# Sliding-window attention and a dropless mixture of experts: rows of a slot turned by VectorE in 32x32 blocks, over buckets with another order of columns

## The chip, the cores and the metric

The kernel runs on one core of a Trainium2 chip. A time is the device time of one execution in microseconds (us). Below, PE is TensorE (its weight loads are listed apart as PEld), DVE is VectorE, ACT is ScalarE, POOL is GpSimd and SP is SyncE, which here only issues DMAs.

## The reference

Everything is in fp32. There are 8 batches of 8 heads with 576 positions of 64 values. Attention is causal and sparse: in heads 0 to 3 a query sees the last 32 keys, in heads 4 to 7 every fourth one of the last 128.

```python
scores = scale * np.matmul(q, k.transpose(0, 1, 3, 2))
mask_plain = (rel >= 0) & (rel < 32)
mask_dil = (rel >= 0) & (rel < 128) & (rel % 4 == 0)
attn = softmax(where(mask, scores, -1e9));  out = attn @ v
```

The heads of one token are put side by side, which makes 4608 rows of 512 values (512 = 8 heads x 64). Each row goes to one of 8 experts, the one with the largest logit, and is weighted with its softmax probability:

```python
logits = x @ w_gate;  expert_idx = np.argmax(logits, axis=1)
gate_w = probs[np.arange(N), expert_idx]
y[rows of e] = np.maximum(x[rows of e] @ w1[e], 0.0) @ w2[e]      # 512 -> 1024 -> 512
return gate_w[:, None] * y
```

## The kernel before

**Attention.** The work is cut into 32 units: for each batch two types of head, and for each type two pairs of heads. A unit turns q and k (`turn`), makes scores in bands of 96 keys (`front`), exponentials on ACT, the division on POOL (`norm`), turns the weights (`weights`, whose tile `eT` DVE copies from PSUM) and sums the values (`summed`). The result `xT` of a unit holds 128 of a token's 512 values, on partitions, by 576 tokens. `row_part` turns it back on PE into rows (`xrow`), and ACT (L574) and DVE (L577) copy these into the tile `rows`, 514 values per token: the 512 values, the weight of the gate and the token's number.

**Routing.** When a batch has ended, `route` finds each token's expert and its rank in it, and POOL scatters the rows with indirect DMAs into `bucket`, a DRAM tensor with a region for each expert. `tables` then computes, for the slots of that stage, which expert a slot has, where its 128 rows begin (`base`) and whether it needs new weights (`new`).

**Slots.** The expert layers run in slots of 128 rows of one expert, up to 41 of them. Two slots, called mixed, hold rows of two experts, in four groups of G = 32. For each slot:

- `fetch_x` reads 128 rows of 514 values from the bucket into the tile `x` (four buffers), with one DMA (four in a mixed slot). SP issues it for the first 26 slots, ACT for later ones; there it is ordered after the last ReLU of ACT (`evicted`).
- `fetch_w` reads the expert's w1 and w2 in four DMAs of 1 MB, on SP's queue, if the expert is new. There are two buffers, and a half is asked for when the slot that used it last has passed the place where it reads it. The list `wanted` fixes the order of the fetches, and `done` counts how far the slots have come.
- `across` turns the slot's rows: four transposes on PE into one PSUM bank, and one copy by DVE to the tile `xt` (two buffers), with the 512 values on partitions in four chunks of 128. It is called for the next slot between the two halves of `ph` (in a mixed slot, in the middle of `py`).
- `ph` is x @ w1 for 8 chunks of 128 hidden values, in two halves; ACT applies the first ReLU and DVE the second. Each half is 16 matmuls of 128x128 by 128 columns, which the trace lists as 32 (L1239).
- `py` is h @ w2, 8 matmuls into 512 columns (16 in the trace, L1271). ACT scales the result with the row's gate (L1282), DVE turns the token number into an integer (L1285) and POOL scatters the rows to the output (L1288).

In a mixed slot the operands change places: `xt` is the stationary one, by groups of 32 columns (`grouped`, L1201), and the hidden rows are turned on PE (`turned_h`).

**Order.** Slots are interleaved with attention by hand. `moe` is a generator that yields the estimated cost of what it has issued (0.93 for the four matmuls of a chunk of ph, 0.88 for a chunk of py, 0.5 for `across`), and `run_slots` at the end of the program lets it run at a rate that makes a stage's slots, `SLOT` each, end with the attention that runs beside them. Within an engine, `tc.issue_after` adds an order where it is wanted: the first DVE instruction of `norm` comes after the last turned tile (`crossed`). Slots from number 36 on are in branches that are only taken if the slot has rows.

Of the kernel before, what the change touches and what calls it, by code (L numbers as in the profile page):

```python
# [12 lines left out]
F32 = mybir.dt.float32  # L13
I32 = mybir.dt.int32
BF16 = mybir.dt.bfloat16
AF = mybir.ActivationFunctionType
# [20 lines left out]
ROW = DM + 2  # L37
# [126 lines left out]
def kernel(  # L164
# [398 lines left out]
    def row_part(b, c, xT):  # L563

        if c == 2:
            rows[b] = pool.tile([TT, NT, ROW], F32, tag="rows", name=f"rows_{b}")
            logits[b] = lpsum.tile([128, TT + REST], F32, tag="logits", name=f"logits_{b}")
            nc.gpsimd.tensor_scalar(
                rows[b][:, :, DM + 1], const("tok", TT), float(b * S), None, op0=OP.add
            )  # L570
        ps, row = bank("xrow", 4, 128), rows[b][:, :, 128 * c : 128 * c + 128]
        for i in range(NT - 1):
            nc.tensor.transpose(ps[:, i], xT[:, TT * i : TT * i + TT], ident)  # L573
        nc.scalar.copy(row[:, 0 : NT - 1], ps)  # L574
        ps = bank("xrow")[0:REST, 0:128]
        nc.tensor.transpose(ps, xT[:, S - REST : S], ident)
        nc.vector.tensor_copy(row[0:REST, NT - 1], ps)  # L577

    def logit_part(b, c, xT):

# [490 lines left out]
    w1s = cpool.tile([128, 2, 4, F], F32, name="w1")  # L1071
    w2s = cpool.tile([128, 2, 8, DM], F32, name="w2")
    mixed = {J0 + at0: i for i, at0 in enumerate(MIX)}
    xs, guards, evicted = {}, ExitStack(), []

    def fetch_x(j):
        b, n, _, basei, _ = where[j]
        x = xs[j] = mpool.tile([128, ROW], F32, tag="x", name=f"x_{j}", bufs=4)
        with ExitStack() as order:


            queue = nc.sync
            if j >= J0 + 2:
                queue = nc.scalar
                if j < SURE:
                    order.enter_context(tc.issue_after(evicted[-1].ins))
            if j in mixed:
                for g in range(4):
                    a = 2 * NMIX + 4 * mixed[j] + g
                    at0 = queue.value_load(  # L1090
                        mix["ints"][:, a : a + 1], min_val=0, max_val=NROWS - G
                    )
                    read_bucket(queue.dma_start(x[G * g : G * g + G], bucket[ds(at0, G), :]), b)
            else:
                at0 = queue.value_load(basei[:, n : n + 1], min_val=0, max_val=E * CAP)
                read_bucket(queue.dma_start(x, bucket[ds(at0, 128), :]), b)

    regs = {}

# [65 lines left out]
    def moe():  # L1165


        def across(j):
            ps = bank("xt", 4, 128)
            for c in range(4):  # L1170
                nc.tensor.transpose(ps[:, c], xs[j][:, 128 * c : 128 * c + 128], ident)  # L1171
            xt = mpool.tile([128, 4, 128], F32, tag="xt", name="xt")
            crossed.append(nc.vector.tensor_copy(xt, ps))  # L1173
            return xt

        late, xt = [], None
        for j in range(NSLOT):
# [5 lines left out]
            if j >= SURE:  # L1183
# [2 lines left out]
                guards.enter_context(tc.If(live[0] > j))  # L1186
                while late:
                    late.pop(0)()
            x = xs[j]
            if xt is None:  # L1190
                xt = across(j)
                yield 0.5
            h = mpool.tile([128, 8, 128], F32, tag="h", name="h")
            w1, w2 = w1s[:, j % 2], w2s[:, j % 2]
            nxt = None
# [1 line left out]
            def grouped(out, lhsT, ws, cols, c, n, j=j):  # L1197

                for g in range(4):
                    mine = slice(G * g, G * g + G)  # L1200
                    nc.tensor.matmul(  # L1201
                        out[mine],
                        lhsT=lhsT[:, mine],
                        rhs=ws[:, (j + (g >= KIND[mixed[j]])) % 2, c, cols],
                        start=c == 0,
                        stop=c == n - 1,
                    )

            def turned_h(hrow, fg):
                ps = bank("ht", 4, 128)  # L1210
                for fi in range(4):
                    nc.tensor.transpose(ps[:, fi], hrow[:, fi], ident)
                (nc.scalar.copy, nc.vector.tensor_copy)[fg](h[:, 4 * fg : 4 * fg + 4], ps)

            hrows = []
            for fg in range(2) if j in mixed else ():
                ph = bank("ph")
                for c in range(4):
                    grouped(ph, xt[:, c], w1s, slice(512 * fg, 512 * fg + 512), c, 4)
                    if (fg, c) == (1, 1):  # L1220
                        turned_h(hrows[0], 0)
                    yield 0.93
                hrow = mpool.tile([128, 4, 128], F32, tag="xt", name="hrow")
                flat = hrow.rearrange("p i f -> p (i f)")
                done[0] = 2 * j + fg + 1
                if fg == 0:
                    evicted.append(nc.scalar.activation(flat, ph, AF.Relu))
                    while late:
                        late.pop(0)()
                else:  # L1230
                    relu = nc.vector.tensor_scalar(flat, ph, 0.0, None, op0=OP.max)
                fetch()
                hrows.append(hrow)
            for fg in range(2) if j not in mixed else ():
                ph = bank("ph", 4, 128)
                for fi in range(4):
                    f = 4 * fg + fi
                    for c in range(4):
                        nc.tensor.matmul(  # L1239
                            ph[:, fi],  # L1240
                            lhsT=w1[:, c, 128 * f : 128 * f + 128],
                            rhs=xt[:, c],
                            start=c == 0,
                            stop=c == 3,
                        )
                    if fi < 3:
                        yield 0.93
                done[0] = 2 * j + fg + 1
                if fg == 0:
                    evicted.append(nc.scalar.activation(h[:, 0:4], ph, AF.Relu))  # L1250
                    while late:
                        late.pop(0)()
                    fetch()
                    yield 0.93
                    if j + 1 in xs:
                        nxt = across(j + 1)
                        yield 0.5
                else:
                    relu = nc.vector.tensor_scalar(h[:, 4:8], ph, 0.0, None, op0=OP.max)  # L1259
                    fetch()  # L1260
                    yield 0.93
            py = bank("py")
            for f in range(8):
                if j in mixed:
                    if f == 2:
                        turned_h(hrows[1], 1)
                    if f == 4 and j + 1 in xs:
                        nxt = across(j + 1)
                    grouped(py, h[:, f], w2s, slice(0, DM), f, 8)
                else:  # L1270
                    nc.tensor.matmul(py, lhsT=h[:, f], rhs=w2[:, f], start=f == 0, stop=f == 7)  # L1271
                if f == 3:
# [6 lines left out]
            else:  # L1279
                y = mpool.tile([128, DM], F32, tag="yo", name="y")  # L1280
                to = mpool.tile([128, 1], I32, tag="to", name="to", bufs=6)
            nc.scalar.activation(y, py, AF.Copy, scale=x[:, DM : DM + 1])  # L1282

            with tc.issue_after(relu.ins):
                nc.vector.tensor_copy(to, x[:, DM + 1 : ROW])  # L1285

            def scatter(y=y, to=to):
                i = nc.gpsimd.indirect_dma_start(  # L1288
# [21 lines left out]
    slots, routing = moe(), []  # L1310
    clock = {"moe": 0.0, "all": 0.0, "owed": 0.0, "rate": 0.0}
    ready = []
    SLOT = 0.5 + 8 * 0.93 + 8 * 0.88


    ATT, BEHIND = 32.0, 12.0
# [77 lines left out]
```

## Time and profile before

| what | value |
|---|---|
| median of 3 runs | 776.44 us (770.65 to 779.24) |
| profiled execution | 830.33 us |
| its span | 828.5 us |
| PE busy | 773.6 us, 93% |
| DVE / ACT / POOL busy | 274.4 / 229.1 / 146.3 us |
| mean granted PE clock | 0.956 |
| moved by DMA | 195.42 MB, mean 236 GB/s |
| slots that ran | 35 ordinary, 2 mixed |

The page gives the busy time of each engine, the chain of work that ended last (followed back from the last instruction to what released it each time), and groups of instructions by line with busy time, mean duration and the idle time ahead of them. Matmuls are pipelined: the duration in a record is longer than the time by which the next one starts, so the time that PE needs for a piece is read from start to start. A tile's own view gives its instructions, what its engine waited for and who waited for the tile.

### The profile page before, as it was taken

The page shows a single profiled execution, that of the slowest core. Times are in us where ns is not written, and L with a number is a line of the kernel's source. Part 1 is how long each engine was busy: PE and PEld are TensorE (multiplying, and loading weights), DVE is VectorE, ACT ScalarE, POOL GpSimd, SP SyncE. Part 2 cuts the span into 40 slices and gives each one's busy share as a digit, 9 for nine tenths or more (in the row PEclk, how much of TensorE's full clock was granted, in tenths as well). Part 3 has the DMA queues.
Part 4 walks back from the last instruction along what each step waited for, and adds up shares of the span by engine and source line. Part 5 has one row for each costly group of instructions (what it writes and reads, how often), then busy time and mean ns, then how long its engine had stood idle before and what let it go on. Part 6 is the DMA issues. An engine that isn't in the chain of part 4 may idle for free.

```text
span 828.5 us, 18147 instructions
## 1 busy us (share of the span) xinstructions
PE 773.6 (93%) x6870; PEld 574.1 (69%) x6870; DVE 274.4 (33%) x963; ACT 229.1 (28%) x853; POOL 146.3 (18%) x142
## 2 busy tenths in 40 slices
PE   6997997998999899989999899969999999999993
PEld 4776775886777677767777677646777466577681
DVE  3674765664343433443341311135110110101010
ACT  4985663552333233222331010000100101000010
POOL 4424333113111311130110200060000000000000
PEclk9998979898999899998999989978999999999997
DMA  7985679998998968796406818978994292883996
GB/s 184 208 194 162 139 187 323 294 264 265 358 269 294 305 189 243 245 303 232 132 26 223 261 59 289 327 241 295 313 335 149 93 317 99 318 313 138 324 312 213
DMA packets 177053, 195.42 MB, mean 236 GB/s; under 512 B 71249, under 2 KB 103137, under 8 KB 176963
## 3 DMA queue, kind: packets, MB, share of 16 engines
q1 hardware_dynamic: 166960, 169.01, 65.8%
q0 software_dynamic: 7248, 21.43, 7.2%
q10 hardware_dynamic: 2754, 3.78, 1.4%
q8 instruction: 57, 0.93, 0.5%
q14 instruction: 34, 0.27, 0.1%
HBM read 216.16 MB, written 21.54 MB: 287 GB/s over the span
## 4 chain that ended last, share of the span: by engine, by line
PE 85%; issue 5%; ACT 5%; DVE 1%; another core or an unknown queue 1%; DMA 1%; POOLq 0%; ACTq 0%; POOL 0%; DVEq 0%
PE ph L1239 31%; PE py L1271 29%; PE xo L469 5%; PE weights L454 3%; PE scores L388 3%; ACT e L425 3%; PE turned L342 2%; PE xt L1171 2%; PE ph L1201 2%; PE py L1201 2%; PE logits L583 2%; PE xrow L573 2%; PE turned L351 2%; DMA k<-in_k_dram 1%
## 5 line engine op out<-in xcount | busy, mean ns | idle before, releaser
L1239 PE MATMUL ph<-xt,w 128*128 128x128 f32 x2240 | 276.4, 280 | 4.1 <-issue 3.1
L1239 PEld LDWEIGHTS ph<-xt,w 128*128 128x128 f32 x2240 | 267.3, 196 | 18.0 <-issue 15.7
L1271 PE MATMUL py<-w,h 128*128 128x512 f32 x560 | 262.5, 609 | 3.9 <-issue 3.9
L1271 PEld LDWEIGHTS py<-w,h 128*128 128x128 f32 x560 | 102.8, 194 | 107.9 <-issue 105.9
L1288 POOL DMA_INDIRECT out_dram<-y,to x35 | 34.8, 993 | 412.0 <-ACT y L1282 326.6
L1173 DVE COPY xt<-xt 128x512 f32<-128x512 f32 x38 | 26.3, 691 | 211.1 <-PE xt L1171 205.8
L1282 ACT ACTIVATE y<-py,x 128x512 f32<-128x512 f32 x35 | 24.0, 687 | 223.0 <-PE py L1271 181.4
L444 POOL TENSOR_TENSOR e<-e,rec 128x864 f32<-128x864 f32 x32 | 52.2, 1631 | 142.2 <-DVE rec L443 121.7
L456 DVE COPY eT<-weights 96x384 f32<-96x384 f32 x96 | 47.3, 545 | 58.6 <-PE weights L454 44.9
L469 PE MATMUL xo<-eT,v 96*64 96x64 f32 (+1 forms) x1216 | 51.6, 233 | 13.7 <-issue 13.6
L469 PEld LDWEIGHTS xo<-eT,v 96*64 96x64 f32 x1216 | 44.1, 144 | 21.0 <-issue 16.6
L425 ACT ACTIVATE e<-e,lo 128x96 f32<-128x96 f32 x144 | 51.8, 362 | 12.0 <-DVE lo L417 10.9
L425 ACT ACTIVATE e<-scores,lo 128x96 f32<-128x96 f32 (+1 forms) x160 | 52.4, 345 | 2.3 <-DVE lo L404 1.9
L239 POOL DMA_INDIRECT bucket<-rows,idx x40 | 39.0, 975 | 56.0 <-DVE idx L671 37.3
L1259 DVE TENSOR_SCALAR h<-ph 128x512 f32<-128x512 f32 x35 | 24.1, 688 | 73.5 <-PE ph L1239 73.5
L334 ACT COPY kT<-turned 128x288 f32<-128x288 f32 x64 | 22.5, 403 | 86.0 <-PE turned L342 44.0
L1250 ACT ACTIVATE h<-ph 128x512 f32<-128x512 f32 x35 | 20.9, 596 | 89.9 <-PE ph L1239 73.7
L454 PE MATMUL weights<-ident,e 128*96 128x128 f32 x288 | 39.3, 281 | 3.0 <-issue 2.0
L454 PEld LDWEIGHTS weights<-ident,e 128*96 128x96 f32 x288 | 32.2, 129 | 10.4 <-issue 8.1
L388 PEld LDWEIGHTS scores<-kT,qT 64*64 64x64 f32 x1152 | 31.8, 143 | 9.7 <-issue 4.0
L388 PE MATMUL scores<-kT,qT 64*64 64x96 f32 x1152 | 36.8, 260 | 1.2 <-ACT kT L334 1.0
L410 DVE TENSOR_TENSOR e<-scores,masks 128x384 f32<-128x384 f32 x64 | 23.0, 399 | 33.7 <-PE scores L388 18.1
(220 smaller groups left out, 612.5 us busy)
## 6 DMA issues: line engine op xcount, KB each, us to landing
w<-in_moe_w_dram SPq DMA_DIRECT2D x164, 1024.0 KB
x<-bucket SPq DMA_DIRECT2D x26, 257.0 KB
v<-in_v_dram SPq DMA_DIRECT2D x32, 192.0 KB
q<-in_q_dram SPq DMA_DIRECT2D x32, 144.0 KB
v<-in_v_dram SPq DMA_DIRECT2D x48, 96.0 KB
k<-in_k_dram SPq DMA_DIRECT2D x28, 144.0 KB
x<-bucket ACTq DMA_DIRECT2D x11, 257.0 KB
q<-in_q_dram SPq DMA_DIRECT2D x14, 192.0 KB
```

What stands on the lines that cost most here:

```text
L239: nc.gpsimd.indirect_dma_start(out=bucket, out_offset=bass.IndirectOffsetOnAxis(ap=idx, axis=0), in_=rows, in_offset=None, bounds_check=NR ...
L388: nc.tensor.matmul(sc[r][64 * c : 64 * c + 64, 96 * (i % 5) : 96 * (i % 5) + 96], lhsT=qT[rows, 64 * j : 64 * j + 64], rhs=kT[rows, first_ ...
L425: nc.scalar.activation(out=e[p0:p1, i], in_=s[:, 96 * (i - i0) : 96 * (i - i0) + 96], func=AF.Exp, bias=lo[p0:p1, i : i + 1], scale=-1.0, ...
L444: return nc.gpsimd.tensor_tensor(out=e, in0=e, in1=rec.unsqueeze(2).broadcast_to([128, 9, 96]), op=OP.mult)
L454: nc.tensor.transpose(tp[0:96, 128 * i : 128 * i + 128], e[:, a + i], ident)
L456: nc.vector.tensor_copy(eT, tp[0:96, 0:384])
L469: nc.tensor.matmul(xo[DH * h : DH * h + DH, at0 : at0 + nq], lhsT=vt[:, 2 * hl + r, j, :] if ty == 0 else vt[:, hl, j, DH * r : DH * r + D ...
L1173: crossed.append(nc.vector.tensor_copy(xt, ps))
L1201: nc.tensor.matmul(out[mine], lhsT=lhsT[:, mine], rhs=ws[:, (j + (g >= KIND[mixed[j]])) % 2, c, cols], start=c == 0, stop=c == n - 1,)
L1239: nc.tensor.matmul(ph[:, fi], lhsT=w1[:, c, 128 * f : 128 * f + 128], rhs=xt[:, c], start=c == 0, stop=c == 3,)
L1271: nc.tensor.matmul(py, lhsT=h[:, f], rhs=w2[:, f], start=f == 0, stop=f == 7)
L1288: i = nc.gpsimd.indirect_dma_start(out=out, out_offset=bass.IndirectOffsetOnAxis(ap=to, axis=0), in_=y, in_offset=None, bounds_check=N - 1 ...
```

## The change

An ordinary slot's rows are turned by DVE, with `nc.vector.transpose`, in place of four transposes on PE and a copy. DVE's transpose turns each block of 32x32 by itself, so the rest of the turning is put into the layout:

- `row_part` writes the columns of a row in another order. Value 128 c + 32 i + d (chunk c, quarter i of the chunk) goes to column 128 i + 32 c + d. A quarter i of all four chunks then lies side by side, 128 values.
- `fetch_x` reads an ordinary slot's rows in four pieces, one for each i: partitions 32 i to 32 i + 31 get the piece i of all 128 rows, as four groups g of 32 rows (partition t of the 32 holds the rows 32 g + t). These are descriptors of 512 bytes. Gate and token number come with a fifth DMA into a tile of their own, `tail`.
- `across` is then one DVE instruction over 128 partitions and 512 columns, SBUF to SBUF. Its result is ordered by group, chunk and row in the group, so `ph` reads its moving operand as four runs of 32 columns with a stride of 128 columns.
- A mixed slot keeps PE's transposes. ACT first puts its columns back into the old order (tile `order`), and its DMAs are eight in place of four.
- The yields of 0.5 for `across` are gone, and so is their share of `SLOT`.

```diff
-        ps, row = bank("xrow", 4, 128), rows[b][:, :, 128 * c : 128 * c + 128]
+        ps = bank("xrow", 4, 128)
+        row = rows[b][:, :, 0:DM].rearrange("p n (i q d) -> p n i q d", i=4, q=4)[:, :, :, c]
         for i in range(NT - 1):
             nc.tensor.transpose(ps[:, i], xT[:, TT * i : TT * i + TT], ident)
-        nc.scalar.copy(row[:, 0 : NT - 1], ps)
+        nc.scalar.copy(row[:, 0 : NT - 1], ps.rearrange("p n (i d) -> p n i d", i=4))
         ps = bank("xrow")[0:REST, 0:128]
         nc.tensor.transpose(ps, xT[:, S - REST : S], ident)
-        nc.vector.tensor_copy(row[0:REST, NT - 1], ps)
+        nc.vector.tensor_copy(row[0:REST, NT - 1], ps.rearrange("p (i d) -> p i d", i=4))
...
-        x = xs[j] = mpool.tile([128, ROW], F32, tag="x", name=f"x_{j}", bufs=4)
+        x = xs[j] = mpool.tile([128, 4, 128], F32, tag="x", name=f"x_{j}", bufs=4)
+        tail = tails[j] = mpool.tile([128, ROW - DM], F32, tag="tail", name=f"tail_{j}", bufs=4)
...
                         mix["ints"][:, a : a + 1], min_val=0, max_val=NROWS - G
                     )
-                    read_bucket(queue.dma_start(x[G * g : G * g + G], bucket[ds(at0, G), :]), b)
+                    read_bucket(
+                        queue.dma_start(
+                            x[G * g : G * g + G].rearrange("t i d -> t (i d)"),
+                            bucket[ds(at0, G), 0:DM],
+                        ),
+                        b,
+                    )
+                    read_bucket(
+                        queue.dma_start(tail[G * g : G * g + G], bucket[ds(at0, G), DM:ROW]), b
+                    )
             else:
                 at0 = queue.value_load(basei[:, n : n + 1], min_val=0, max_val=E * CAP)
-                read_bucket(queue.dma_start(x, bucket[ds(at0, 128), :]), b)
+                for i in range(4):
+                    part = bucket[ds(at0, 128), 128 * i : 128 * i + 128]
+                    read_bucket(
+                        queue.dma_start(
+                            x[G * i : G * i + G], part.rearrange("(g t) d -> t g d", t=G)
+                        ),
+                        b,
+                    )
+                read_bucket(queue.dma_start(tail, bucket[ds(at0, 128), DM:ROW]), b)
...
         def across(j):
-            ps = bank("xt", 4, 128)
-            for c in range(4):
-                nc.tensor.transpose(ps[:, c], xs[j][:, 128 * c : 128 * c + 128], ident)
-            xt = mpool.tile([128, 4, 128], F32, tag="xt", name="xt")
-            crossed.append(nc.vector.tensor_copy(xt, ps))
+            xt = mpool.tile([128, 4, 4, G], F32, tag="xt", name="xt")
+            if j in mixed:
+                order = pool.tile([128, S], F32, tag="qT", name="order", bufs=2)[:, 0:DM]
+                order = order.rearrange("p (q i d) -> p q i d", q=4, i=4)
+                nc.scalar.copy(order, xs[j].rearrange("p i (q d) -> p q i d", q=4))
+                ps = bank("xt", 4, 128)
+                for c in range(4):
+                    nc.tensor.transpose(
+                        ps[:, c], order[:, c].rearrange("p i d -> p (i d)"), ident
+                    )
+                nc.vector.tensor_copy(
+                    xt.rearrange("p g c t -> p c g t"), ps.rearrange("p c (g t) -> p c g t", g=4)
+                )
+                return xt
+            crossed.append(
+                nc.vector.transpose(
+                    xt.rearrange("p g c t -> p (g c t)"), xs[j].rearrange("p g d -> p (g d)")
+                )
+            )
             return xt
...
-            x = xs[j]
+            x = tails[j]
             if xt is None:
                 xt = across(j)
-                yield 0.5
...
-                        lhsT=lhsT[:, mine],
+                        lhsT=lhsT(g),
...
-                    grouped(ph, xt[:, c], w1s, slice(512 * fg, 512 * fg + 512), c, 4)
+                    grouped(ph, lambda g: xt[:, g, c], w1s, slice(512 * fg, 512 * fg + 512), c, 4)
...
-                            ph[:, fi],
+                            ph[:, fi].rearrange("p (g t) -> p g t", g=4),
                             lhsT=w1[:, c, 128 * f : 128 * f + 128],
-                            rhs=xt[:, c],
+                            rhs=xt[:, :, c],
...
                         nxt = across(j + 1)
-                        yield 0.5
...
-            nc.scalar.activation(y, py, AF.Copy, scale=x[:, DM : DM + 1])
+            nc.scalar.activation(y, py, AF.Copy, scale=x[:, 0:1])
...
-                nc.vector.tensor_copy(to, x[:, DM + 1 : ROW])
+                nc.vector.tensor_copy(to, x[:, 1:2])
...
-    SLOT = 0.5 + 8 * 0.93 + 8 * 0.88
+    SLOT = 8 * 0.93 + 8 * 0.88
```

## The prediction

> **What bounds the kernel now.** I read the chain that ended last first. It names the engine that has no time to give away.
>
> ```profile
> PE 85%; issue 5%; ACT 5%; DVE 1%; another core or an unknown queue 1%; DMA 1%; POOLq 0%; ACTq 0%; POOL 0%; DVEq 0%
> PE ph L1239 31%; PE py L1271 29%; PE xo L469 5%; PE weights L454 3%; PE scores L388 3%; ACT e L425 3%; PE turned L342 2%; PE xt L1171 2%; PE ph L1201 2%; PE py L1201 2%; PE logits L583 2%; PE xrow L573 2%; PE turned L351 2%; DMA k<-in_k_dram 1%
> ```
>
> TensorE (PE) makes 85% of the chain, and the transposes that the change removes (xt, L1171) are 2% of it: they are on the path. How long are they there? The matmul records overlap, so I don't use their durations. I use the starts, in two neighbouring slots of the last stage (columns: start us, us):
>
> ```profile
> 668.99 3.84 PE L1239 MATMUL ph<-xt,w 128*128 128x128 f32 x32
> 672.66 0.60 PE L1171 MATMUL xt<-ident,x 128*128 128x128 f32 x4
> 673.10 3.74 PE L1239 MATMUL ph<-xt,w 128*128 128x128 f32 x32
> 676.67 3.60 PE L1271 MATMUL py<-w,h 128*128 128x512 f32 x8
> ...
> 609.66 3.57 PE ph L1239 x32
> 613.67 3.57 PE ph L1239 x32
> 617.25 6.87 PE py L1271 x16
> 624.11 3.57 PE ph L1239 x32
> ```
>
> The four transposes start at 672.66 and the next matmuls at 673.10: 0.44 us. The chain says the same: 609.66 + 3.57 = 613.23, next start 613.67. A slot is 3.57 + 0.44 + 3.57 + 6.87 = 14.45 us, with no gap.
>
> Third, who waits for whom, for the rest of the slot: does PE wait for the tiles, or for weights?
>
> ```profile
> L1171 PEld LDWEIGHTS xt<-ident,x x152: 137/141/230, 129.7 to 804.7; 128*128 128x128 f32 x152
> L1171 PE MATMUL xt<-ident,x x152: 272/273/421, 129.7 to 804.9; 128*128 128x128 f32 x152
>   issue: 1.7, 2
> ...
> L1173 DVE COPY xt<-xt x38: 678/692/693, 130.6 to 805.2; 128x512 f32<-128x512 f32 x38
>   PE xt L1171: 205.8, 34
> ...
> SPq L1115 <- PE py L1271: 137.5, 48, 4.4
> SPq L1115 <- PE ph L1239: 122.4, 43, 7.2
> ```
>
> 152 transposes are 38 turned tiles. In front of them PE sat idle for 1.7 us in all, and never for a row fetch. The copy of VectorE (DVE) waits for PE, not PE for it. The queue that fetches weights (SPq, L1115) waits 260 us for PE to free buffers: the weights are held up by PE, not PE by them.
>
> Fourth, the stretches (columns: length, busy time of PE, its weight loads, DVE, ACT and POOL, clock, DMA share, GB/s):
>
> ```profile
> 130.00:200.00 70.00, 62.48 (x702) 50.19 (x699) 39.53 (x142) 29.55 (x118) 20.23 (x18) 0.94 0.94 288
> 200.00:300.00 100.00, 96.97 (x899) 77.67 (x898) 40.26 (x129) 32.76 (x123) 17.60 (x16) 0.94 0.96 298
> 400.00:540.00 140.00, 136.94 (x993) 103.26 (x992) 33.19 (x121) 24.55 (x69) 15.93 (x15) 0.98 0.57 186
> 566.00:650.00 84.00, 84.00 (x499) 62.57 (x498) 12.40 (x51) 7.70 (x12) 5.84 (x6) 1.00 0.72 250
> ```
>
> From 200 us on PE is full in every stretch; DVE has 60% to 85% of its time free. The DMA engines are nearly full from 130 to 300 us and have room later.
>
> [...] No DVE transpose is in this trace. [...]
>
> **The change, part by part.**
>
> *Removed from PE.* 38 turned tiles less the two of mixed slots, which keep their transposes: 36 x 0.44 = 15.8 us. All of it is on PE's path, and PE is full, so all of it counts. Next in line are the second half of ph, whose operand and weights are there already, and, one slot later, weights: SP waits for PE there, so a faster PE lets them start sooner. In the first slot PE also waited for the copy ("DVE xt" 1.3 us); I count no gain for that.
>
> *Moved to DVE.* The copy from PSUM (36 x 0.69 us) becomes a transpose from SBUF. [...] I take 0.7. [...] Queued behind it on DVE are the reductions, eT copies and the second ReLU; PE waits for these. What is new is that DVE itself waits for the fetched rows.
>
> *Fetches.* An ordinary slot has five DMAs in place of one. Issue: 0.36 us each, so 4 x 0.36 = 1.4 us more on SP (26 slots) or ACT's queue (11). Ahead of the use there is room: rows 2 and 3 are issued at 170.0 us and the third tile is turned at 181.5; in the last stage the issue precedes the use by over 10 us. What is pushed back on SP are weight fetches, which now wait 260 us in all for PE. On ACT the first ReLU is done before the issue; its output is needed some 3 us later. In a mixed slot 1.4 us may delay the copy of the turned h by some tenths: 0.2 us for both. Engine time: before 128 x 102 / 16 = 0.82 us per slot; after 512 x 31 / 16 = 0.99, and 128 packets of 8 bytes at 9 ns (four-byte packets in the trace) = 0.07. That is 0.25 us more per slot, hidden.
>
> *Bucket order.* ACT (L574, 591 ns) and DVE (L577, 279 ns) write runs of 32 values at a stride. In the trace ACT takes 686 ns for 288 elements written one by one at a stride (L490) and 403 in one run (L334), so 1 ns per element at the worst: +0.5 us x 32 copies on an engine that is 28% busy. With runs of 32 I take 0 on the path.
>
> *Strided operand.* ph's moving operand is now four runs of 32 columns. No matmul of this trace reads so. Nothing (weight loads run back to back beside these matmuls at 114 ns, so the operand isn't alone in setting the pace) to some 12 ns each; a gain has no source. I take 0.
>
> *Mixed slots.* Two ACT copies of 0.6 to 0.7 us come before PE's transposes. If ACT does them while the preceding ph runs, they cost nothing; if they queue behind the ReLU, PE stands 0.6 + 0.7 + about 0.2 = 1.5 us, twice. Between 0 and 3 us; I take 1.2, since the rows are there early.
>
> *Yields.* The transposes' 0.5 leaves the interleaving's accounts on both sides; I take 0, plus or minus 2 us.
>
> **Sum.** -15.8 + 1.2 + 0.2 = -14.4 us. The profiled execution takes 830.33 us (span 828.5): after, 816. It is 54 us longer than the median of the runs, 776.44. It holds stretches (at 198, 280, 371, 475 and 545 us) where PE, DVE and POOL all crawl at once with no releaser and the clock halves after; I take them to be of the profile, and transposes hardly lie in them. So the saving carries over in microseconds: 776.4 - 14.4 = **762 us**.
>
> **Rivals.**
> *Less gain for full DMAs.* From 130 to 300 us the DMA share is 0.94 to 0.96, and eight tiles are turned. If transfers set the pace there, 8 x 0.44 = 3.5 us are not won and 8 x 0.25 = 2 us are added: 767 to 768; with the issue delays up to 771. Against it: PE is full there.
> *DVE stands at rows that haven't landed: slower.* DVE works in order, and a transpose is ready as soon as rows come, so it may be put well ahead of its need. Rows queued behind four weight fetches wait as long as these take (13.2 us at 457 us). At each of seven stage starts DVE could stand 4 us and, with eT copies and ReLUs behind it, PE too: 7 x 4 = 28 us, 790 us. It decides once DVE's waits beyond PE's cover pass 14.4 us in sum. Against it: the issue leads of over 10 us.
> *The strided operand costs.* 2240 matmul records: 15.8 us / 2240 = 7 ns each eat the gain; 12 ns give +27 us, 789.
> *The 0.44 us is not given back*, as another wait fills it: 776. Against it: the gapless slots.
>
> **How the numbers follow.** Forecast 0.68; full DMAs 0.12; DVE stands 0.09; strided operand 0.06; nothing 0.05. A change under 1% can't be told from none here. Faster: 0.68 and about half of 0.12, 0.74; slower: 0.15; the rest 0.11. The forecast's own range is 757 to 768 (mixed slots 0 to 3, yields, and the runs' own spread, 770.65 to 779.24). With the full-DMA case and no gain the range is 756 to 776, which leaves the slower cases outside.
>
> **What would show it.** Right: no xt transposes but eight, for the mixed slots; ordinary slots of 14.0 us in the last stage; DVE transposes near 0.7 us, waiting for DMAs but with no PE waits on eT or h growing. Wrong: ph's 32 matmuls over 3.57 us (strided operand); PE waiting for weights between 130 and 300 us (DMAs); long DVE waits for row fetches with PE waiting for DVE behind them; PE standing over 1.5 us at each mixed tile.

## The result, and the profile after

The changed kernel takes **780.44 us** (median of 20 runs, 777.16 to 784.53), the kernel before, in 20 runs beside them, 775.51 us. The ratio is 1.0073, with an interval of 1.0055 to 1.009. The forecast was 762 us with a range of 756 to 776; I had a gain of 14.4 us, and there is a loss of 5. The profiled execution took 781.88 us.

The removed work did go. Ordinary slots of the last stages, from the chain that ended last of the changed kernel (start us, us, what):

```profile
551.89 7.14 PE ph L1279 x64
559.04 6.87 PE py L1310 x16
565.91 7.14 PE ph L1279 x64
573.05 6.87 PE py L1310 x16
...
593.93 3.57 PE ph L1279 x32
597.50 0.44 PE xt L1200 x4
597.94 2.12 PE ph L1279 x19
```

A slot is 14.01 us in place of 14.45, and ph's 64 matmuls take 7.14, twice the 3.57 of before: the strided operand costs nothing. DVE's turning, from the groups of instructions (busy us, mean ns, then the idle time before them):

```profile
L1209 DVE STREAM_TRANSPOSE xt<-x 128x512 f32<-128x512 f32 x36 | 25.3, 705 | 11.9 <-DMA x<-bucket 11.5 <-DVE to_staged L1324 0.2
```

But the chain as a whole reads otherwise. Its shares by engine, changed kernel:

```profile
PE 73%; DMA 7%; SPq 5%; ACT 5%; issue 3%; DVE 3%; another core or an unknown queue 1%; ACTq 0%; POOLq 0%; POOL 0%; DVEq 0%
```

Nothing of SP and 1% of DMA stood in the chain that I predicted from (2% and 3% in another profile of the same kernel, below); now they are 12%. Most of it lies between 100 and 270 us. Pieces of the chain from 203 to 245 us:

```profile
203.37 0.44 SPq L312
203.81 0.04 issue
203.86 0.44 SPq L312
...
205.76 0.19 SPq L1138
205.95 0.05 issue
206.11 6.39 DMA w<-in_moe_w_dram
212.50 0.14 issue
212.63 2.05 PE ph L1279 x8
...
228.04 4.11 SPq L299
232.20 2.51 SPq L299
234.75 1.64 SPq L299
236.44 0.19 SPq L1138
236.63 0.05 issue
236.78 7.38 DMA w<-in_moe_w_dram
```

This is what the prediction had the other way round: SP works through its list (L299 and L312 are attention's loads of v), then comes to a weight fetch, and PE's next matmuls start when those weights land. In this part of the program PE follows SP.

From here on I use one measure, the start of the matmul of `tables` at the third and the fourth stage, worked out from the records of each trace, and the start of the last matmul of py:

| kernel (profiled run) | third tables | fourth tables | between | fourth to last py |
|---|---|---|---|---|
| before, profiled again | 175.1 | 249.6 | 74.5 | 510.6 |
| changed | 176.6 | 265.8 | 89.2 | 499.6 |
| turning alone, one DMA | 174.2 | 248.4 | 74.2 | 494.9 |

The loss is between the third and fourth tables: 14.7 us, with 1.5 ahead of them. From there to the last py the changed kernel wins back 11.0. These are single profiled executions; the three kernels that were profiled twice, later and on other chips, repeat the time between third and fourth tables within 1 us, while whole runs of one kernel lie some 6 us apart (757.99 to 763.57 for the turning alone).

### The profile page after: what moved, and what is told of

It reads as the page before. It is cut to its first block, busy times and chain, and to the rows that moved or that the text cites. A ratio compares the mean times of both kernels' runs of the same rounds, so it can differ in the third digit from the quotient of the medians.

```text
span 780.0 us, 18347 instructions
## 1 busy us (share of the span) xinstructions
PE 735.9 (94%) x6726; PEld 544.3 (70%) x6726; DVE 272.8 (35%) x963; ACT 229.3 (29%) x855; POOL 146.3 (19%) x142
## 4 chain that ended last, share of the span: by engine, by line
PE 73%; DMA 7%; SPq 5%; ACT 5%; issue 3%; DVE 3%; another core or an unknown queue 1%; ACTq 0%; POOLq 0%; POOL 0%; DVEq 0%
PE ph L1279 28%; PE py L1310 26%; DMA w<-in_moe_w_dram 4%; PE xo L469 4%; ACT e L425 3%; PE scores L388 3%; PE weights L454 2%; PE ph L1239 2%; PE py L1239 2%; DMA q<-in_q_dram 2%; PE turned L351 2%; SPq L299 2%; PE xrow L575 1%; PE logits L585 1%; PE turned L342 1%
## 5 line engine op out<-in xcount | busy, mean ns | idle before, releaser
L1279 PE MATMUL ph<-xt,w 128*128 128x128 f32 x2240 | 270.3, 279 | 10.8 <-DMA w<-in_moe_w_dram 10.8
L1279 PEld LDWEIGHTS ph<-xt,w 128*128 128x128 f32 x2240 | 262.4, 195 | 25.1 <-issue 23.9
L1310 PE MATMUL py<-w,h 128*128 128x512 f32 x560 | 254.9, 596 | 4.4 <-ACT h L1290 2.7
L1310 PEld LDWEIGHTS py<-w,h 128*128 128x128 f32 x560 | 100.6, 190 | 104.0 <-issue 97.9
L1321 ACT ACTIVATE y<-py,tail 128x512 f32<-128x512 f32 x35 | 24.0, 684 | 209.6 <-PE py L1310 176.1
L469 PE MATMUL xo<-eT,v 96*64 96x64 f32 (+1 forms) x1216 | 43.4, 224 | 0.2 <-issue 0.2
L469 PEld LDWEIGHTS xo<-eT,v 96*64 96x64 f32 x1216 | 38.7, 138 | 4.8 <-ACT dl L632 0.4
L332 DVE TENSOR_SCALAR qT<-turned 128x288 f32<-128x288 f32 x64 | 26.3, 447 | 34.3 <-PE turned L351 22.6
L425 ACT ACTIVATION_READ_ACCUMULATOR e<-scores,lo 128x1 f32 (+1 forms) x160 | 33.4, 209 | 0.0
```

Source lines behind the costliest of these rows:

```text
L332: nc.vector.tensor_scalar(out, in_, -SCALE, None, op0=OP.mult)
L425: nc.scalar.activation(out=e[p0:p1, i], in_=s[:, 96 * (i - i0) : 96 * (i - i0) + 96], func=AF.Exp, bias=lo[p0:p1, i : i + 1], scale=-1.0, ...
L469: nc.tensor.matmul(xo[DH * h : DH * h + DH, at0 : at0 + nq], lhsT=vt[:, 2 * hl + r, j, :] if ty == 0 else vt[:, hl, j, DH * r : DH * r + D ...
L1279: nc.tensor.matmul(ph[:, fi].rearrange("p (g t) -> p g t", g=4), lhsT=w1[:, c, 128 * f : 128 * f + 128], rhs=xt[:, :, c], start=c == 0, st ...
```

## The experiments

Two theories, and a third that the durations above already speak against. **Work** (A in the expectations): the fetch's own cost, wherever it appears (more DMAs, or more and smaller packets), delays the weights on SP. **Order** (C): the yields that went with the transposes shifted the interleaving. B puts the cost into the turning itself, the strided operand or the order of DVE's work. Under A there are again three: the packets' engine time (A2), SP's time to issue (A1a), and the completion semaphores (A1b); A1 is the last two together. SP's and ACT's DMAs raise eight semaphores in turn in the trace of before (107 and 109 to 115), and 450 of SP's 459 DMAs have a wait for the last use of their own.

### The parts, one by one

First the kernel before once more, as a profile on the same chip as the next three.

> The kernel before, unchanged, for a profile without the stretches in which everything crawls. If these belong to the profile of that one execution, the span is about 775 us, PE waits for weights little between 100 and 270 us, and the stages can be compared with those of the changed kernel. If they belong to the kernel, the span is again about 828 us.

It took 774.8 us, with a span of 773.0 and a granted clock of 0.992. So the profiled execution of 830.33 us from which I predicted is not what a profile makes of this kernel; more on that below.

Then the five-DMA fetch without the turning:

```diff
-                read_bucket(queue.dma_start(x, bucket[ds(at0, 128), :]), b)
+                for i in range(4):
+                    part = bucket[ds(at0, 128), 128 * i : 128 * i + 128]
+                    read_bucket(queue.dma_start(x[G * i : G * i + G, 0:DM]..., part...), b)
+                read_bucket(queue.dma_start(x[:, DM:ROW], bucket[ds(at0, 128), DM:ROW]), b)
```

> The kernel before, but an ordinary slot's rows are fetched with the five DMAs of the changed kernel (four pieces with packets of 512 bytes, and the tail), and then turned by PE as before. The columns land in the wrong places, so that the rows are not those of the reference. Theory A (the five DMAs on SP's queue push the weight fetches back while that queue and the DMA engines are full, up to about 270 us): the loss of the changed kernel, some 5 us, plus the 15 to 16 us that its PE saves, appear here as a pure loss: 793 to 797 us, ratio about 1.025. Theory B (the fetch is harmless, the cost is in the turning, in the strided operand or in the order of DVE's work): 775 to 778.

787.8 us, ratio 1.0133 (1.0092 to 1.0175): a clear loss, but only about half of what theory A had. Of it, 7 us lie ahead of the third tables (182.2 for 175.1), where PE itself stood 5.3 us at rows, and 3 between third and fourth (77.4 for 74.5). And the turning without the fetch, on the changed kernel:

```diff
-                for i in range(4):
...
-                read_bucket(queue.dma_start(tail, bucket[ds(at0, 128), DM:ROW]), b)
+                read_bucket(queue.dma_start(x, bucket[ds(at0, 128), :]), b)
```

> The changed kernel, but an ordinary slot's rows are fetched with one DMA of whole rows, as before; DVE turns the blocks of what is there, which leaves the values in the wrong arrangement. Theory A: the forecast comes true without the five DMAs: 760 to 764 us, ratio about 0.982. Theory B: 780 or a little below.

761.11 us, ratio 0.9792 (0.975 to 0.9833): 16.4 us below the kernel before, where the terms for PE's 36 tiles sum to 15.8. So the turning does all that was forecast for it, and the fetch takes it away. The two don't add: -16.4 and +10.3 make -6, and the changed kernel is at +5. My reading, which is argued from the chain above and not shown by a run, is that the quicker PE asks for weights sooner, where SP is late with them.

The yields back in the changed kernel:

```diff
+                yield 0.5
...
-    SLOT = 8 * 0.93 + 8 * 0.88
+    SLOT = 0.5 + 8 * 0.93 + 8 * 0.88
```

> The changed kernel with the yields of 0.5 for the turning, and their share of SLOT, as before. Theory A: no difference from the changed kernel, 778 to 783. Theory C (the pace is what went wrong: without the yields the slots run ahead and ask for weights at a worse time): 762 to 770.

777.37 us, ratio 1.0 (0.9978 to 1.0022), against 1.0073: 0.7%, some 5 us, more than theory A had (none) and less than C. Its third to fourth tables still take 89.9 us (174.1 to 264.0). Order matters somewhat, and isn't the main cause.

### Packets or DMAs

Turning with four DMAs of 32 whole rows (2056-byte packets), on the turning alone:

```diff
-                read_bucket(queue.dma_start(x, bucket[ds(at0, 128), :]), b)
+                part = bucket[ds(at0, 128), :]
+                for i in range(4):
+                    read_bucket(queue.dma_start(x[G * i : G * i + G], part[G * i : G * i + G]), b)
```

> The changed kernel, but an ordinary slot's rows come in four DMAs of 32 whole rows (packets of 2056 bytes, no tail of its own); DVE turns what is there, in the wrong arrangement. Theory A1 (it is the number of DMAs: SP and ACT use eight completion semaphores between them in the trace, a DMA waits for the one that it will raise, so that small DMAs behind weights use up the eight): most of the loss is there, 773 to 780 us, and SP waits for earlier DMAs by tens of us. Theory A2 (it is the packets: 640 small ones in place of 128 load the DMA engines): 761 to 764, as with one DMA.

776.46 us, 1.001 (0.9991 to 1.0029): with as many bytes in as many packets as one DMA has, three DMAs more cost 17 us (0.0218 of 776). And the reverse, the changed kernel's 512-byte packets in one DMA, beside the one for the tail:

```diff
-                for i in range(4):
...
+                part = bucket[ds(at0, 128), 0:DM]
+                read_bucket(queue.dma_start(x, part.rearrange("r (g d) -> r g d", g=4)), b)
```

> The changed kernel, but the values of an ordinary slot's rows come in one DMA whose packets are 512 bytes (the tile keeps a gap of 4 values behind each 128), with the tail's DMA beside it: two DMAs with the packets of the changed kernel, and values in the wrong arrangement. Theory A1: 762 to 767 us. Theory A2: about 778 to 781, as the changed kernel.

768.35 us, 0.9887 (0.9851 to 0.9923): 7 us over the turning alone, with one DMA more, the tail's, and 512 small packets. So it is the number of DMAs, far more than the packets. How the 7 us part between the one DMA and the packets this run alone does not say; the table of SP's time below leaves little for the packets.

### Off SP's queue

The first 26 slots' DMAs on POOL's queue (`queue = nc.gpsimd` for `nc.sync`), and then all slots' there.

> The changed kernel whole, but the five DMAs of each of the first 26 slots are issued by POOL, whose DMAs raise other semaphores and stand in another queue; later slots keep ACT. Theory A1: SP's waits for earlier DMAs go back to those of the kernel before and most of the saving appears: 760 to 767 us, unless POOL's own issue (0.6 to 1 us each, five per slot) delays its multiplication in the attention, then 768 to 775. Theory A2: about 780, since the packets are the same.

> As the last one, but the rows of all slots are issued by POOL. Theory A1: 1 to 3 us faster than with ACT for the late slots if the semaphores that ACT's five DMAs take from SP matter there too, otherwise the same; slower if POOL's scatters of the output stand before the fetches. Theory A2: about 780.

779.13 us, 1.0043 (1.0024 to 1.0062), and 784.96 us, 1.0119 (1.0086 to 1.0151). The first is what A2 forecast, but not for its reason: a new wait takes the place of the old. POOL scatters the rows into the buckets, in order; a fetch stands behind that, and so the rows come late. Of the first of the two, POOL's wait for its scatters from 90 to 200 us, then DVE's waits for rows and PE's for DVE over the whole span (us in all, times, longest):

```profile
POOL x L1114 <- DMA bucket<-rows,idx: 8.7, 1, 8.7
...
DVE xt L1209 <- DMA x<-bucket: 34.2, 6, 14.6
PE lg L604 <- DVE lgs L600: 11.3, 3, 10.2
PE weights L454 <- DVE e L410: 10.7, 1, 10.7
```

The two DVE instructions that PE waits for, 10.2 and 10.7 us, come behind turnings that stood at rows for 9.0 and 14.6 us. This is the prediction's rival of DVE standing at rows: it doesn't slow the changed kernel (below), but it does slow this one. The third tables come at 196.5 us in place of 176.6; the fourth follow 74.1 us later, as with the turning alone, but SP also had 20 us more for its list by then.

Its windows (length, busy time of PE, weight loads, DVE, ACT, POOL, clock, DMA share, GB/s) show the loss moved forward, to where PE stands behind DVE, and PE full afterwards:

```profile
100.00:200.00 100.00, 77.40 (x986) 62.15 (x986) 55.92 (x193) 42.72 (x174) 40.22 (x49) 0.86 0.92 255
200.00:300.00 100.00, 100.00 (x1002) 76.71 (x995) 43.34 (x143) 36.79 (x140) 34.91 (x45) 1.00 1.02 297
```

### Two kinds of chip, found by the way

The next runs were to part SP's time from the semaphores. They came to two other chips, and there the kernel before took **828 us** in the median (822 to 831), unprofiled runs included, where on the chips so far it took 776. Three edits:

```diff
 # tail on POOL: on the changed kernel
+                if j < J0 + 2:
+                    at0 = nc.gpsimd.value_load(basei[:, n : n + 1], min_val=0, max_val=E * CAP)
+                    queue = nc.gpsimd
                 read_bucket(queue.dma_start(tail, bucket[ds(at0, 128), DM:ROW]), b)
 # SP busy: on the turning alone
+                if queue is nc.sync:
+                    for _ in range(3):
+                        at0 = queue.value_load(basei[:, n : n + 1], min_val=0, max_val=E * CAP)
                 read_bucket(queue.dma_start(x, bucket[ds(at0, 128), :]), b)
 # hybrid: on the changed kernel with the yields back
+                if j < 8:
+                    read_bucket(queue.dma_start(x, bucket[ds(at0, 128), :]), b)
+                    return
...
-            if j in mixed:
+            if j in mixed or j < 8:
```

> The changed kernel whole, with one of the five DMAs, the tail, issued by POOL for the first 26 slots: four on SP. Theory A1 (number of DMAs on SP and their semaphores): part of the loss goes, 772 to 778 us; the run with four DMAs of whole rows took 776. If the tail's 128 packets of 8 bytes were the cost themselves (theory A2), 780.

> The run with DVE's turning and one DMA of whole rows (761.1 us, values in the wrong arrangement), with three more loads of a register on SP ahead of each row fetch of the first 26 slots: about 2 us of SP's time each, as four more DMAs take to issue, but no semaphore and no transfer. If SP's issue time is the cost (theory A1a): 770 to 777 us. If it is the completion semaphores, which small DMAs hold while they stand behind weights (A1b): 761 to 764.

> Computes what the reference asks. The changed kernel, but the first eight slots fetch whole rows with one DMA and are turned by PE (ACT puts the columns in order first, as in a mixed slot), and the yields are those of the kernel before. Theory A (the whole loss lies in the slots before about 266 us): that stretch is as in the kernel before and the saving of the later slots stays, 28 x 0.44 = 12 us less 1 to 3 for the mixed slots and the late fetches: 763 to 767 us. If the loss also arises later: 770 or more.

The ratios were 0.9771 (0.9726 to 0.9815), 0.9806 (0.9758 to 0.9854) and 0.9995 (0.9973 to 1.0016), and nothing could be said before the changed kernel itself had run on such a chip. It did next, beside the same three on another one of the kind:

> The changed kernel itself, beside the three kernels of the last set, which ran on a chip where the kernel before takes 828 us. On a chip where that takes 776 us: 780, ratio about 1.007. On the other chip: theory A expects the same loss between the second and the fourth stage, so that the ratio lies near or above 1 and well above that of the run with SP kept busy; if it is 0.98 there, the loss isn't the kernel's but depends on the chip.

> The changed kernel with the tail issued by POOL, again. Theory A1: below the changed kernel of this set by 3 to 8 us. Theory A2 (packets): equal to it.

> DVE's turning, one DMA of whole rows and about 2 us more of SP's time per fetch, again. Issue time as the cause (A1a): within 5 us of the changed kernel of this set. Semaphores as the cause (A1b): 12 us or more below it, ratio to the kernel before about 0.98.

> The first eight slots turned by PE after one DMA, again. Theory A: 763 to 767 us where the kernel before takes 776, ratio about 0.985, and 15 us below the changed kernel. On the other chip it was 0.9995, which would say that ACT's copies or their wait cost there what the fetch saves.

| kernel | us | ratio to before (827.68) |
|---|---|---|
| changed | 811.23 | 0.9808 (0.9771 to 0.9846) |
| tail on POOL | 806.76 | 0.9759 (0.9703 to 0.9814) |
| SP busy | 808.41 | 0.9774 (0.9735 to 0.9813) |
| hybrid | 826.45 | 0.9988 (0.9971 to 1.0005) |

The same change **wins 1.9% here and loses 0.7% there**. The gain is 16.4 us, against 14.4 forecast. The first three don't differ by more than their intervals, so the number of DMAs on SP makes no difference that can be seen on these chips; the turning alone did not run there. The hybrid wins nothing: its first eight slots are turned on PE behind an ACT copy, and it keeps the yields. Of the 15 us to the changed kernel 12 lie ahead of the third tables (204.6 us for 192.6); which of the two takes them was not separated.

Where does the stretch's loss go? Third tables, fourth tables, between, fourth to last py:

| kernel, chip of this kind | third | fourth | between | to last py |
|---|---|---|---|---|
| before (the profile of the prediction) | 193.4 | 273.7 | 80.3 | 541.3 |
| changed | 192.6 | 271.0 | 78.4 | 522.4 |

And the chain's shares of the changed kernel there:

```profile
PE 80%; issue 5%; ACT 4%; DVE 4%; DMA 3%; another core or an unknown queue 2%; SPq 1%; ACTq 0%; POOLq 0%; POOL 0%; DVEq 0%
```

SP and DMA are 4% of it, not 12%. PE gets to the third tables 16 us later than on the other chips (192.6 for 176.6), in time that SP can use for its list. The fourth tables then come at 271.0, nearly where SP's list lets them come on the other chips too, 265.8; for the kernel before the same two places are 273.7 and 249.6. So there SP's later weights are covered by a later PE. This fits all marks, but is argued: no run slowed PE alone. Nor is it known what makes these chips slower. Over the runs of the kernel before, the mean granted clock is 0.956 to 0.963 there and 0.985 to 0.995 on the others, 3% apart, while the time is 6.6% longer. If all time scaled with the clock, that would be half of it.

### SP's time or the semaphores

The same three edits, on a chip where the kernel before takes 776.63 us:

> The version with one DMA of whole rows per slot, and some 2 us of register loads on SP at each fetch that stand for the issue of four more DMAs without sending them. If it is SP's time that the four more DMAs cost, this gives back most of what they cost where the kernel before takes some 776 us: 0.99 to 1.00 of before. If it is that they hold completion semaphores, it stays near the version with one DMA: 0.975 to 0.982. Where the kernel before takes some 828 us it says nothing (0.975 to 0.98 either way).

> The changed kernel with the fifth DMA of each early slot on POOL's queue and its semaphores, four pieces on SP. If the number of DMAs that share SP's semaphores is what costs, one less in five gives a fifth to a half of the loss back where the kernel before takes some 776 us: 0.995 to 1.004 of before, against 1.007 of the changed kernel. If POOL's place in order costs as much as it saves: 1.005 to 1.01. Where the kernel before takes some 828 us: 0.976 again.

> The changed kernel, but its first 8 slots fetch whole rows with one DMA, ScalarE puts them in order and TensorE turns them, and the weight yields of before are back. If the loss of the changed kernel where the kernel before takes some 776 us lies only in the early fetches' four more DMAs, this gives most of it back: 0.98 to 0.99 of before. If the later slots' five DMAs cost as well, or TensorE waits for ScalarE's copies as it did where the kernel before takes some 828 us: 1.00 to 1.01. There: 0.999 again.

**SP busy:** 773.42 us, 0.996 (0.9943 to 0.9976). One DMA per slot, nothing sent beyond it, and 13 us (0.0168 of 776) of the changed kernel's 22 us over the turning alone (0.0281) are there (with the intervals of both ratios, 10 to 17). SP's time as such costs them. SP's queue around one fetch shows the size, from the end of a weight fetch to the start of the next: for the turning alone, SP busy and the changed kernel, in this order (start us, us, line, count):

```profile
220.25 0.61 SPq L1121 DMA_DIRECT2D w<-in_moe_w_dram  x1
221.93 0.37 SPq L1102 DMA_DIRECT2D x<-bucket  x1
223.86 0.38 SPq L1121 DMA_DIRECT2D w<-in_moe_w_dram  x1
```

```profile
232.66 1.22 SPq L1124 DMA_DIRECT2D w<-in_moe_w_dram  x1
236.69 0.37 SPq L1105 DMA_DIRECT2D x<-bucket  x1
238.98 0.39 SPq L1124 DMA_DIRECT2D w<-in_moe_w_dram  x1
```

```profile
236.78 0.46 SPq L1138 DMA_DIRECT2D w<-in_moe_w_dram  x1
238.60 1.92 SPq L1114 DMA_DIRECT2D x<-bucket  x4
240.78 0.36 SPq L1119 DMA_DIRECT2D tail<-bucket  x1
242.72 0.39 SPq L1138 DMA_DIRECT2D w<-in_moe_w_dram  x1
```

3.0 us, 5.1 and 5.5: SP spends 2.1 us more in the stand-in and 2.5 in the changed kernel. There it takes 0.51 to 0.58 us from one row DMA to the next, of which 0.32 to 0.36 are the DMA's record. Third to fourth tables take 74.2, 85.0 and 89.2 us. Four such fetches lie in that stretch and two more just ahead of it. Not all are alike, so here are all six, summed from the records of each trace in the same way: from the end of SP's DMA ahead of the rows to the start of the one behind them, less the 14.2 us of the turning alone. Beside it stands the stretch, less its 74.2 us.

| kernel | SP at six fetches, us more | third to fourth tables, us more |
|---|---|---|
| one DMA of small packets, and the tail | 8.8 | 10.6 |
| SP busy | 10.6 | 10.8 |
| four DMAs of whole rows | 12.2 | 12.0 |
| tail on POOL | 12.9 | 12.9 |
| changed | 17.2 | 15.0 |

From one DMA per fetch to five, and for large packets and small, the stretch grows by what SP spends, within 2.2 us: here a us on SP is about a us of the kernel. PE's windows from 200 to 266 us show what becomes of it, for the kernel before, the turning alone, SP busy and changed:

```profile
200.00:266.00 66.00, 65.19 (x634) 52.14 (x633) 28.12 (x99) 22.38 (x81) 14.09 (x13) 1.00 0.96 307
```

```profile
200.00:266.00 66.00, 66.00 (x636) 52.76 (x636) 27.92 (x98) 22.10 (x79) 15.66 (x14) 1.00 0.97 300
```

```profile
200.00:266.00 66.00, 59.80 (x573) 47.76 (x565) 25.93 (x90) 18.59 (x62) 12.80 (x11) 0.95 0.96 300
```

```profile
200.00:266.00 66.00, 59.02 (x548) 47.55 (x540) 22.89 (x65) 20.57 (x75) 8.96 (x7) 0.92 0.97 288
```

The DMA share is 0.96 or 0.97 in all four, so it doesn't tell them apart; PE's busy time falls by 6 us as soon as SP is busier.

**Tail on POOL:** 776.57 us, 1.0017 (0.9996 to 1.0037), below the 1.0073 of the changed kernel. One DMA less on SP gives 4 us back. It takes time and a semaphore off SP at once, and so doesn't part the theories by itself.

**Hybrid:** 773.92 us, 0.9958 (0.9941 to 0.9974), a part of the expected gain only. Its third to fourth tables take 73.6 us (189.2 to 262.8), as with the turning alone. But the third tables come 13 us later than in the changed kernel, which also gives SP time, so that the stretch is no clean test here. They come later in part behind ACT's copies; what PE waited for from 90 to 210 us:

```profile
PE xt L1212 <- ACT order L1209: 8.9, 2, 4.8
```

What stays open: 22 us less the 13 that the stand-in shows. The stand-in is short of the changed kernel by 6.6 us of SP's time in the table, so most of the other 9 can be more of the same. That leaves little for the semaphores. I had suspected that rows hold them, which queue behind weights. Over the whole span SP's waits for rows do grow, from 20.1 us with the turning alone (line L1121) to this in the changed kernel:

```profile
SPq L1138 <- DMA x<-bucket: 50.1, 9, 16.6
```

But these 50.1 us all lie behind 540 us. From the third to the fourth tables such waits sum to 1.3 us with the turning alone and to none in the changed kernel. SP's waits for weights grow there, from 7.0 to 13.3 us, while its waits for PE fall from 7.0 to 2.8, and all its waits together stay as they are (16.2 and 16.7). Whether those 6 us for weights cost anything was not measured by itself. From the fourth tables on, SP busy and the changed kernel both take some 5 us more than the turning alone (500.2 and 499.6 us for 494.9), which no run explains.

No kernel that computes the reference wins as much on the first kind of chip as the turning alone does, which leaves the values in the wrong places. Of those run on both kinds, the changed kernel with its tail on POOL is the best compromise: 0.976 on the one, no difference on the other.

## Why the prediction was wrong

**The step that failed: fetches, "What is pushed back on SP are weight fetches, which now wait 260 us in all for PE".** The 260 us are a sum over the span. I took it as slack everywhere, and it lies in the later stages: 0.9 us of it between 130 and 200 us and 12.3 between 200 and 300. The profile of before had the answer, in SP's waits from 193 to 274 us alone:

```profile
SPq L312 <- DMA w<-in_moe_w_dram: 8.1, 4, 3.5
SPq L1115 <- PE ph L1239: 4.2, 1, 4.2
SPq L312 <- PE xo L469: 1.8, 1, 1.8
```

All waits for PE in those 80 us sum to 9.0 us; an even spread of the 260 us over the span would give 25. On the chips of the result it is less (kernel before, 175 to 250 us):

```profile
SPq L280 <- PE weights L454: 2.0, 1, 2.0
SPq L272 <- PE py L1271: 1.8, 1, 1.8
```

with 2.1 us for turned and 0.5 for xt, 6.4 us of 75. There were 1.4 us of issue per fetch in my working, and I set them at nothing. The changed kernel has 2.5 in the fetch shown and 17.2 over six, since register work and short waits come with each DMA, and the stretch with these fetches is 15.0 us longer than with one DMA each.

**The step that failed second: the carrying over.** I took the crawling stretches to be "of the profile" and so carried the saving in microseconds to 776. The runs show them to belong to a kind of chip: there the kernel before takes 828 us unprofiled, and 773.0 us of span with a profile elsewhere. The page of the changed kernel there also has 13.0 us of idle time without a releaser ahead of xo, for 0.2 on the chips of the result. I had read the trace of one kind and predicted the time of the other. For the kind that the trace came from, the sum came out: 16.4 us (12.7 to 19.0 by the interval) against 14.4. In part that is luck: SP spends some 16 us more at the same six fetches there too (31.4 for 15.7), and the 260 us, of which 9.0 lie there, were no reason for nothing to be lost.

**Right:** 0.44 us per tile and 36 tiles (the turning alone gave 16.4 us for 15.8, with an interval of 13 to 19); DVE's transpose, 0.705 us measured for 0.7 taken, which was my estimate: the trace that I had shows none, and a copy of that size takes 0.69 there; the strided operand, 0 and 0 (the 12 ns were a guess of mine that no run shows); engine time of small packets, for which I had the means of that trace on SP's queue, 102 ns for a packet of 2056 bytes and 31 for one of 512: the experiment with 512-byte packets shows it to be at most a small part (third to fourth tables 10.6 us longer, SP's time 8.8). DVE's turning has no term in the sum: the rest of ph and py, 3.57 + 6.87 = 10.4 us, lies ahead of its use, and PE stood behind one only, for 3.4 us (below).

**Sizes:** mixed slots, 1.2 us taken, 0 measured (597.50 follows 593.93 + 3.57 without a gap, and the other mixed slot is the same). Yields, 0 plus or minus 2 taken, 5 us measured.

**Rivals:** "Less gain for full DMAs" named the right place, 130 to 300 us, and PE does wait for weights there, but its price was too low: it had 2 us of transfer and "issue delays" of 3, and the loss is SP's time. "Against it: PE is full there" holds from 200 us on (96.97 of 100); from 130 to 200 my own line had 62.48 of 70. DVE stood 11.5 us at rows, in seven waits, and PE only once behind it:

```profile
who waited for it (us, times):
  PEld ph L1279: 3.4, 1
```

so that rival, which was mine for "slower", isn't the mechanism of the changed kernel; it is that of the version with its DMAs on POOL.

## What to carry to other kernels

A queue's waits, summed over the span, say nothing of the stage where an edit lands: ask for the waits in that stretch, and count what the queue does itself between them, register loads included. Splitting a DMA can cost more than what it feeds saves, with the bytes and even the packets the same: here it cost as much as the issuing queue's time at it (four DMAs of whole rows, third to fourth tables: 12.0 us for 12.2). And moving it to another queue needs the same count there, since it then stands behind that queue's work (on POOL's, 8.7 us at once behind the scatters). Where a trace and the median of the runs are 7% apart, they may stand for two machines: a forecast from the one is then a forecast for that one.

## What the runs showed of the hardware

- Chips differ: the kernel before takes 776 us on three chips and 828 on two, with a mean granted clock of 0.985 to 0.995 and 0.956 to 0.963; the change has a ratio of 1.0073 on the one kind and 0.9808 on the other.
- Three more DMAs of the same packets, on SP's queue at 26 fetches and on ACT's at the later ones, cost 17 us (ratios to before of 0.9792 and 1.001).
- DVE turns a 128x512 tile of fp32 in blocks of 32 in 705 ns, about as long as its copy of that size from PSUM took (691 ns).
- A moving operand in four runs of 32 columns takes the same time as one of 128 in a row: 7.14 us for the 64 matmul records of a slot, twice 3.57.
- On POOL's queue the record of a DMA of rows is 572 ns long in the median, on SP's 333 ns; with the register work between them SP takes 0.51 to 0.58 us from one to the next.
- SP's time counts though nothing is sent: three register loads more at each of 26 fetches, 2.1 us at the one shown, cost 13 us (0.9792 to 0.996).
